# Splitting seven of the fourteen block products of a fused attention and MLP kernel a second time

## The chip, the cores and the metric

The kernel runs on one core of a Trainium2 chip. The core has five engines that run side by side and wait for each other through semaphores: TensorE (PE, matmuls, with its weight loads shown as PEld), VectorE (DVE), ScalarE (ACT), GpSimd (POOL) and SyncE (SP). Each takes its instructions strictly in the order of its own queue, so an instruction that waits holds up all that stand behind it. In this kernel POOL and SP mostly issue transfers. The metric is the device time of one execution in microseconds. Before the change it is 744.53 us, the median of three runs (744.47 to 747.11).

## The reference

The input x has 2048 rows of 1024 numbers in bf16. The output mixes an attention branch and an MLP branch row by row:

```
g = sigmoid((x * gate_w).sum(-1))                  # one number per row
a = attention(x @ wqkv) @ wo                       # 32 heads of 32; each row looks at 8 rows, 2 apart
b = (gelu(x @ w_gate) * (x @ w_up)) @ w_down       # 3584 hidden columns
out = g * a + (1 - g) * b
```

Both branches end in a product with a weight matrix. The kernel joins the two: it stacks the 3584 hidden columns, scaled by 1-g, on the 1024 attention columns, scaled by g, and w_down on wo. So the last stage is one product of 2048 x 4608 by 4608 x 1024.

## The kernel before

**Products by seven.** All large products use the scheme of Strassen in Winograd's form: a product of matrices cut 2 x 2 needs seven block products instead of eight, with sums and differences of blocks formed beforehand and of results afterwards. The last stage cuts each half of the rows (`down(0)` and `down(1)`, 1024 rows each) into left blocks A11, A12, A21, A22 of 512 rows by 2304 columns, and the weights into R11, R12, R21, R22 of 2304 by 512. A block lies in SBUF as 18 rows of 128 x 512. The formed right blocks are T1 = R12-R11, T2 = R22-T1, T3 = R22-R12 and T4 = R21-T2. On the left, S = A21+A22, then S-A11 (called S2 in the change), then A12-S2; A11 becomes A11-A21. One `down` multiplies, in this order: A11 R11, A12 R21, S T1, S2 T2, (A12-S2) R22, (A11-A21) T3, A22 T4. Each is 4 groups (`j`) of 18 matmuls of 128 x 128 by 128 x 512, one group per PSUM bank; `XT` and `VT` name the two sets of four banks.

**The stages in front.** A *unit* is one such product by seven in the earlier stages, of 28 matmuls, and ends on DVE with an addition (L399). Units 0 and 1 are of the MLP, units 2 (`Q0`) to 17 make queries and keys, the next eight the values, the rest gate and up projections. The attention runs on DVE beside the units: products of queries and keys (`qk_mult`, L593), a sum on PE (`reduce_mm`), the softmax, and the weighting of the values (`pv_all`, "PV"), with products (L732) and folds (L739). Query and key pieces at the edge of a half are kept in memory and done later (`spill`). The R combinations T1 to T4 are made in `t_forms` (L835), 36 additions of 1024 elements, and stored to `t_d`.

**Order of the work.** The order on each queue is fixed when the program is built. For each unit, `run_bg` hands out DVE work from background tasks: each step yields its cost, a unit grants about 4.8 us, the task with the smallest priority number goes first, and a task that yields `None` sleeps for one unit. `at` and `at_end` tie calls to a unit; `due` forces a task's end. The hook at `TFE` finishes `t_forms` and calls `load_v`, the load of the value weights for `sums_v` (L542). When `pv_all` is done, it calls `pre_down_2`, which loads A12 and R21. At the start of the last stage `pre_down_3` loads rows 12 and 13 of A11 and A12, the last hidden columns to be made, and `loads` the later blocks as their buffers (`plan`, ten buffers) come free. All these loads are issued by SP.

**DVE in the last stage.** `scale_task` (L867) scales the 12 hidden rows that aren't scaled yet, three instructions of 2048 elements; `comb_task` (L874) forms a combination of blocks, four of 2048 and one of 1024. S-A11 is formed per `j` (L970). Results go through `u2` and `qs`, sums held in SBUF in f32, and out with `add_out` (L937).

Of the kernel before, what the change touches and what calls it, by code (L numbers as in the profile page):

```python
# [67 lines left out]
def kernel(  # L68
# [64 lines left out]
    with tc.manual_schedule(engines={mybir.EngineType.PE, mybir.EngineType.DVE, mybir.EngineType.Activation,  # L133
# [500 lines left out]
        def spill(s):  # L634
            accs, ps = [], []
            temps = [prod_tile() for _ in range(2)]

            def mult(t, dst):
                qk_mult(dst, qb[s][:, t, :], kb[s][:, t, HALO:HALO + AC])

            def add(g, t):
                TT(out=accs[g], in0=accs[g], in1=temps[t % 2], op=ALU.add)  # L642

            for g in range(NT // QG):
                accs.append(prod_tile())
                mult(QG * g, accs[g])
                yield 1.14
                for t in range(1, QG):
                    mult(QG * g + t, temps[t % 2])
                    yield 1.14  # L650
                    if t > 1:
                        add(g, t - 1)
                        yield 1.14
                add(g, QG - 1)
                yield 1.2
            slotq.append(lambda: spill_reduce(s, accs))
# [11 lines left out]
        def softmax(a, cnt, b0, e):  # L668
# [14 lines left out]
            yield 0.55 * cnt + 0.05  # L683
            front.add(a)
            bg(softmax_back(a, cnt, ee, e4, sw, m, bc), 3, now[0] + 1)

        def softmax_back(a, cnt, ee, e4, sw, m, bc):
            nc.scalar.activation(out=ee, in_=ee, func=ACT.Exp, scale=scale)  # L688
            yield None
            while a // BPS not in gated:  # L690
# [25 lines left out]
        def pv_all():  # L716
# [5 lines left out]
            for i, a in enumerate(PVO):  # L722
                if i + 1 < NBLK:
                    while PVO[i + 1] not in ready:
                        yield None
                    pv_load(PVO[i + 1], i + 1)
                if i == 0:
                    yield None
                v, ab, o_ = vb[i % 2], ab_[i % 2], ob_[i % 2]
# [50 lines left out]
        due(Q0 + NT + 1, bg(late_form3(), 1, Q0 + 8))  # L780
        TFE = Q0 + 14
        due(Q0 + 2 * NT, bg(sums_v(), 2, TFE + 1))
        for s in range(2):
# [3 lines left out]
        QE = Q0 + 2 * NT  # L787
        at_end(QE + 1, lambda: (spill_load(0), spill_load(1)))
        bg(spill(0), 4, QE + 3)
        bg(spill(1), 4, QE + 3)  # L790
        bg(pv_all(), 5, QE + 3)

# [38 lines left out]
        def t_forms():  # L831
            for q in range(NQ):
                r11, r12, r21, r22 = tf[q % 3]
                for o_, a, b_ in ((r11, r12, r11), (r12, r22, r12), (r22, r22, r11), (r21, r21, r22)):
                    TT(out=flat(o_), in0=flat(a), in1=flat(b_), op=ALU.subtract)  # L835
                    yield 0.64
                for k, t in enumerate((r11, r22, r12, r21)):
                    nc.gpsimd.dma_start(out=t_d[k][:, NP * q:NP * q + NP, :], in_=t)
                if q + 3 < NQ:
                    tf_load(q + 3)  # L840

        at(Q0 + 1, lambda: [tf_load(q) for q in range(3)])
        tft = bg(t_forms(), 6, Q0 + 2)
        at(TFE, lambda: (tft.finish(), load_v()))

        plan = [dict(A11=4, R11=5, A12=2, R21=3, A21=6, A22=0, S=8, T1=1, T2=9, R22=7, T3=5, T4=3),
                dict(A11=6, R11=1, A12=8, R21=9, A21=2, A22=4, S=0, T1=7, T2=5, R22=3, T3=1, T4=9)]
        u2 = regf(R_U2, 4 * SC).rearrange("p (j n) -> p j n", j=4)
# [60 lines left out]
        def loads(s, *names):  # L909
            B = Bs(s)  # L910
            for k in names:
# [4 lines left out]
                else:  # L916
                    load_T(B[k], int(k[1]))

        def down(s):
            B = Bs(s)  # L920
            last = s == 1
            eng = nc.sync if last else nc.gpsimd
            base = s * SUP
            XT, VT = (6, 7, 0, 1), (5, 2, 3, 4)

# [5 lines left out]
            def emit(ot, c, nh, j):  # L931
                r0 = base + c * SC + j * P
                eng.dma_start(out=o2[r0:r0 + P, nh * SC:(nh + 1) * SC], in_=ot)

# [7 lines left out]
            VP = [bank(VT[j]) for j in range(4)]  # L942
            rest = pieces(scale_task(A21, s, 1, 0, NE_), scale_task(A22, s, 1, 0, NE_), comb_task(S, A21, A22, ALU.add))
            for j in range(4):
                if j > 1 or last:
                    mm(XP[j], A11, B["R11"], j, True)
                else:
                    mm(XP[j], A11, B["R11"], j, True, 0, NK - 2)
                    yield
                    if j == 1:  # L950
                        for jj in range(2):
                            mm(XP[jj], A11, B["R11"], jj, True, NK - 2, NK)
                            nc.scalar.copy(out=u2[:, jj, :], in_=XP[jj])
                if j > 1 or last:
                    nc.scalar.copy(out=u2[:, j, :], in_=XP[j])  # L955
                take(rest, 3)
            run(rest)
            loads(s, "T3")
            for j in range(4):
# [3 lines left out]
                emit(ot, 0, 0, j)  # L963
            loads(s, "T4")
            for j in range(4):
                mm(VP[j], S, B["T1"], j, True)
                nc.scalar.copy(out=qs[:, j, :], in_=VP[j])
            for j in range(4):
                js = slice(j * P, (j + 1) * P)
                TT(out=S[:, :, js], in0=S[:, :, js], in1=A11[:, :, js], op=ALU.subtract)  # L970
            run(comb_task(A12, A12, S, ALU.subtract), comb_task(A11, A11, A21, ALU.subtract))
            if not last:
                loads(1, "A11", "R11")
            for j in range(4):
                mm(XP[j], S, B["T2"], j, True)
                TT(out=u2[:, j, :], in0=XP[j], in1=u2[:, j, :], op=ALU.add)
                TT(out=qs[:, j, :], in0=qs[:, j, :], in1=u2[:, j, :], op=ALU.add)
            if not last:
                loads(1, "A12", "R21")
            for j in range(4):  # L980
                mm(VP[j], A12, B["R22"], j, False)
                add_out(VP[j], u2[:, j, :], 0, 1, j)
            rest = pieces()
            if not last:
                loads(1, "A21", "T1")
                rest = pieces(scale_task(Bs(1)["A11"], 1, 0, 0, NE_), scale_task(Bs(1)["A12"], 1, 0, 0, NE_))
            for j in range(4):
                mm(XP[j], A11, B["T3"], j, True)
                add_out(XP[j], qs[:, j, :], 1, 1, j)
                take(rest, 1)  # L990
            if not last:
                loads(1, "A22", "T2")
            for j in range(4):
                mm(XP[j], A22, B["T4"], j, False)
                add_out(XP[j], u2[:, j, :], 1, 0, j)
                take(rest, 1)
            if not last:
                loads(1, "R22")
            run(rest)
# [4 lines left out]
        def run_last(b):  # L1004
# [9 lines left out]
            prv.p4()  # L1014
            loads(0, "A22", "T1", "T2", "R22")
            for t_ in list(tasks):
# [59 lines left out]
```

## Time and profile before

| | |
|---|---|
| profiled execution | 744.29 us, span 742.5 us |
| TensorE busy | 724.4 us (98%) |
| VectorE busy | 571.5 us (77%) |
| ScalarE busy | 290.9 us (39%) |
| last stage's matmuls (L928) | 1008 issued, 988 recorded, 216.8 us busy |
| last stage, first matmul | 520.40 us |
| data moved | 140.72 MB, 190 GB/s over the span |

The page shares out the busy time of each engine. Its slices cut the span in 40 equal parts with the busy share in tenths. The chain that ended last is followed back from the last instruction, at each step to what released it, so it names the bound. Matmuls are pipelined: a mean of 379 ns for one is the time from its start to its end, and the spacing of a run of them is shorter. Lines of the timeline give start, duration in us, engine, line, operation, output<-input, and how many; a bracket gives the idle time before and what ended it. A line of a table of stretches gives, after the stretch, its length, and the busy time and number of instructions of PE, PEld, DVE, ACT and POOL, then the granted clock, the share of the transfer engines, and GB/s.

### The profile page before, as it was taken

To read this page: it belongs to the slowest core of one execution; us is meant where nothing else is said; L and a number is where in the kernel's file an instruction comes from. 1 tells how busy PE (TensorE), PEld (TensorE's weight loads), DVE (VectorE), ACT (ScalarE), POOL (GpSimd) and SP (SyncE) were. 2 spreads that over 40 slices of the span, in tenths; PEclk is the share of its full clock that TensorE was granted. 3 is DMA by queue.
4 is the path that set the end of the run, shared out by engine and by line. 5 is a ranking of instruction groups with operands and counts; after the bars stand their busy time and mean duration, and the time that the engine had idled before them with its cause. 6 is when DMAs were issued, how large, how long until landed. Compare 5 with 4: busy or idle time off the path is not lost.

```text
span 742.5 us, 9336 instructions
## 1 busy us (share of the span) xinstructions
PE 724.4 (98%) x3498; PEld 356.1 (48%) x3567; DVE 571.5 (77%) x622; ACT 290.9 (39%) x500; POOL 110.8 (15%) x196
## 2 busy tenths in 40 slices
PE   8999999889999999999999999999999999999998
PEld 4466566545544444444444444444444444444443
DVE  3699999898999899999999999995555533606411
ACT  4554445335457655555555555555111000110000
POOL 1234456222211010101010000100010011000000
PEclk9999999999999999999999999999999999999999
DMA  9977784853225526534444743548898799750011
GB/s 280 269 192 248 259 289 143 290 172 115 99 94 145 176 68 197 172 107 152 141 142 152 232 144 114 169 139 273 280 400 325 253 359 396 276 201 30 15 36 36
DMA packets 117486, 140.72 MB, mean 190 GB/s; under 512 B 18704, under 2 KB 101296, under 8 KB 116416
## 3 DMA queue, kind: packets, MB, share of 16 engines
q1 hardware_dynamic: 104128, 101.00, 42.1%
q0 software_dynamic: 13024, 38.59, 15.5%
q8 instruction: 28, 0.46, 0.3%
q10 hardware_dynamic: 288, 0.52, 0.2%
q14 instruction: 18, 0.15, 0.1%
HBM read 98.01 MB, written 39.99 MB: 186 GB/s over the span
## 4 chain that ended last, share of the span: by engine, by line
PE 87%; DVE 5%; issue 1%; ACT 0%; DMA 0%; POOL 0%; another core or an unknown queue 0%; DVEq 0%
PE banks L362 56%; PE banks L928 29%; DVE arena L593 3%; PE banks L598 1%; DVE arena L399 1%; DVE arena L459 1%; DMA gblk<-g_d 0%; DVE arena L642 0%; DVE arena L835 0%; ACT L688 0%; DVE arena L542 0%; PE banks L278 0%; DVE arena L937 0%; ACT arena L688 0%
## 5 line engine op out<-in xcount | busy, mean ns | idle before, releaser
L362 PE MATMUL banks<-arena 128*128 128x512 bf16 x2137 | 472.5, 379 | 11.4 <-DVE arena L399 7.8
L362 PEld LDWEIGHTS <-arena 128*128 128x128 bf16 x2184 | 240.4, 111 | 242.9 <-issue 14.8
L928 PE MATMUL banks<-arena 128*128 128x512 bf16 x988 | 216.8, 379 | 1.1
L928 PEld LDWEIGHTS <-arena 128*128 128x128 bf16 x1008 | 98.6, 98 | 118.9
L399 DVE TENSOR_TENSOR arena<-banks,arena 128x1024 bf16<-128x1024 f32 x78 | 95.2, 1220 | 21.9 <-PE banks L362 17.0
L385 ACT COPY arena<-banks 128x512 f32<-128x512 f32 x78 | 45.8, 587 | 130.8 <-PE banks L362 130.8
L370 ACT CAST arena<-banks 128x512 bf16<-128x512 f32 x102 | 59.8, 586 | 45.1 <-PE banks L362 42.8
L732 DVE TENSOR_TENSOR arena<-arena 128x2048 bf16<-128x2048 bf16 x64 | 76.9, 1219 | 0.4
L593 DVE TENSOR_TENSOR arena<-arena 128x2048 bf16<-128x2048 bf16 x64 | 74.7, 1217 | 0.1
L739 DVE TENSOR_TENSOR arena<-arena 128x2048 bf16<-128x2048 bf16 (+2 forms) x96 | 73.9, 775 | 1.1
L937 DVE TENSOR_TENSOR arena<-banks,arena 128x512 bf16<-128x512 f32 x24 | 16.6, 692 | 67.6 <-PE banks L928 67.6
L256 POOL DMA_DIRECT2D h_d<-arena x28 | 20.1, 718 | 253.5 <-DVE arena L252 209.0
L392 ACT COPY banks<-banks 128x512 f32<-128x512 f32 x78 | 44.5, 571 | 26.6 <-PE banks L362 18.4
L380 ACT COPY banks<-banks 128x512 f32<-128x512 f32 x78 | 45.0, 577 | 13.8 <-PE banks L362 12.4
L970 DVE TENSOR_TENSOR arena<-arena 128x2304 bf16<-128x2304 bf16 x8 | 10.9, 1359 | 42.4 <-PE banks L928 39.9
L319 DVE TENSOR_TENSOR arena<-arena 128x1024 bf16<-128x1024 bf16 x60 | 38.6, 685 | 0.5
L368 ACT ACTIVATE arena<-banks 128x512 bf16<-128x512 f32 x54 | 32.2, 597 | 15.2 <-PE banks L362 14.3
L867 DVE TENSOR_TENSOR arena<-arena,omgrep 128x2048 bf16<-128x2048 bf16 x24 | 28.1, 1217 | 11.3 <-DMA arena<-h_d 11.3
L252 DVE TENSOR_TENSOR arena<-arena 128x2048 bf16<-128x2048 bf16 x28 | 34.0, 1216 | 3.3 <-ACT arena L370 1.9
L955 ACT COPY arena<-banks 128x512 f32<-128x512 f32 x6 | 3.5, 587 | 81.8 <-PE banks L928 81.8
L874 DVE TENSOR_TENSOR arena<-arena 128x2048 bf16<-128x2048 bf16 (+1 forms) x30 | 31.2, 1111 | 0.1
L407 ACT ACTIVATE arena<-arena 128x1024 bf16<-128x1024 bf16 x27 | 28.3, 1049 | 0.0
(76 smaller groups left out, 301.0 us busy)
## 6 DMA issues: line engine op xcount, KB each, us to landing
arena<-t_d SPq DMA_DIRECT2D x8, 2304.0 KB, 13.7
h_d<-arena POOLq DMA_DIRECT2D x28, 512.0 KB, 4.0
arena<-in_B_w_down_dram SPq DMA_DIRECT2D x6, 1792.0 KB, 14.0
arena<-h_d SPq DMA_DIRECT2D x6, 1792.0 KB, 13.5
t_d<-arena POOLq DMA_DIRECT2D x36, 256.0 KB, 4.5
arena<-in_B_w_gate_dram SPq DMA_DIRECT2D x15, 512.0 KB, 5.2
arena<-in_B_w_up_dram SPq DMA_DIRECT2D x15, 512.0 KB, 4.4
arena<-in_B_w_down_dram SPq DMA_DIRECT2D x28, 256.0 KB, 5.8
```

Of the source, the lines that this page charges most:

```text
L252: TT(out=flat(G), in0=flat(G), in1=flat(U), op=ALU.mult)
L319: TT(out=o_, in0=a, in1=b_, op=op)
L362: self.pe = nc.tensor.matmul(ps, lhsT=self.L[form](kt), rhs=rhs[:, kt, :], start=(start and kt == 0), stop=(kt == HK - 1), skip_group_chec ...
L370: nc.scalar.copy(out=o_, in_=i_)
L380: nc.scalar.copy(out=self.Y, in_=self.X)
L385: nc.scalar.copy(out=self.p5s, in_=self.V)
L392: nc.scalar.copy(out=self.Z, in_=self.Y)
L399: TT(out=self.T[:, :, c2s], in0=pair, in1=self.p5s.rearrange("p (o n) -> p o n", o=1).to_broadcast([P, 2, SC]), op=ALU.add)
L593: TT(out=dst, in0=q.rearrange("p (o s) -> p o s", o=1).to_broadcast([P, NWIN, AC]), in1=_win_ap(k, [[-DIL, NWIN], [1, AC]]), op=ALU.mult)
L732: TT(out=prod2[(t // 2) % 2][:, t % 2], in0=ab, in1=_win_ap(v[:, t, HALO:HALO + AC], [[SJ, NJ], [-DIL, NWIN], [1, SJ]]), op=ALU.mult)
L739: TT(out=out_, in0=h(0), in1=h(1), op=ALU.add)
L928: nc.tensor.matmul(ps, lhsT=L[:, i, j * P:(j + 1) * P], rhs=R[:, i, :], start=(start and q == 0), stop=(q == NK - 1), skip_group_check=not ...
```

## The change

Seven of the 14 block products are themselves done by seven: S T1, S2 T2 and A11 T3 in both halves, and A11 R11 in the second. `level2` cuts a left block into quarters of 256 rows by 1152 columns and a right one into 1152 by 256. One product is then 7 x 2 groups of 9 matmuls with 256 columns. `forms_L` and `forms_R` build its eight sums on DVE, four each, in two further buffers (L5 and R5, and so on). The results of the seven add up in place in PSUM: ACT copies quarter results between the halves of banks, one result (`p5d`) goes through SBUF and is added by DVE, and `zero_left` clears the left halves first. S2 is formed as A22-A11 from the already changed A11 and takes A21's buffer; before it was S-A11 in S's own. Before, A22 T4 was added up in the banks that held A11 T3. Now it gets the other banks, VT, and DVE adds A11 T3's banks to `u2` and `u2` to the result. Around it the loads, the buffers, and in the earlier stages the order of the background tasks are arranged anew: `t_forms` stops at unit 14 and goes on after the value units with a priority ahead of PV, `load_v` is called one unit earlier, `spill` waits for the query-key products, the softmax's exponential is a task of its own. The out-stores of the second half go through POOL but for the last block.

```
         def spill(s):
-            accs, ps = [], []
+            while reduced[0] < 2 * NT:
+                yield None
+            accs = []
...
+            bg(softmax_exp(a, cnt, ee, e4, sw, m, bc), 0, now[0] + 1)
...
                 if i == 0:
+                    pv_task[0].prio = 5
+                    tasks.sort(key=lambda t_: t_.prio)
                     yield None
...
-        TFE = Q0 + 14
-        due(Q0 + 2 * NT, bg(sums_v(), 2, TFE + 1))
+        TFE = Q0 + 13
+        due(Q0 + 2 * NT, bg(sums_v(), 2, TFE + 2))
...
-        bg(pv_all(), 5, QE + 3)
+        pv_task = [bg(pv_all(), 4.2, QE + 3)]
...
         def t_forms():
-            for q in range(NQ):
+            q = 0
+            while q < NQ:
+                if now[0] == TFE - 1 and tf_open[0]:
+                    tf_open[0] = False
+                    while now[0] < NQKV + 1:
+                        yield None
+                    for q_ in range(q, min(q + 3, NQ)):
+                        tf_load(q_)
+                    yield None
...
-        at(TFE, lambda: (tft.finish(), load_v()))
...
+        def tf_close():
+            while tf_open[0] and not tft.done:
+                tft.step()
+            tft.prio = 4.5
+            tasks.sort(key=lambda t_: t_.prio)
+            load_v()
+
+        at_end(TFE - 1, tf_close)
...
+        def forms_L(f, b):
+            f = quads(f)
+            q = lambda kh, h: quarter(b, kh, h)
+            for o_, a, b_, op in ((f[:, 0], q(0, 1), q(1, 1), ALU.add), (f[:, 1], f[:, 0], q(0, 0), ALU.subtract),
+                                  (f[:, 2], q(0, 0), q(0, 1), ALU.subtract), (f[:, 3], q(1, 0), f[:, 1], ALU.subtract)):
+                TT(out=o_, in0=a, in1=b_, op=op)
+                yield 1.3
...
+        def level2(bk, L, R, lf, rf):
...
+            cp = lambda d, s_: nc.scalar.copy(out=d, in_=s_)
+            prod(0, 0, lq(0, 0), rq(0, 0), lambda j: cp(c(1, 1, j), c(0, 0, j)))
+            prod(0, 0, lq(0, 1), rq(1, 0))
+            prod(1, 0, lf[:, 0], rf[:, 0], lambda j: cp(p5d[:, j, :], c(1, 0, j)))
+            prod(1, 1, lf[:, 1], rf[:, 1], lambda j: cp(c(0, 1, j), c(1, 1, j)))
+            prod(1, 1, lf[:, 2], rq(0, 1), lambda j: cp(c(1, 0, j), c(1, 1, j)))
+            prod(0, 1, lf[:, 3], rq(1, 1))
+            for i in (1, 0):
+                TT(out=two_banks(bk, i, 1), in0=two_banks(bk, i, 1), in1=p5d, op=ALU.add)
+            prod(1, 0, lq(1, 1), rf[:, 2])
...
         def down(s):
...
+            if last:
+                run(scale_task(A12, s, 0, 0, NE_))
+                level2(XT, A11, B["R11"], B["L1"], B["R1"])
...
+                loads(s, "T2")
+                run(scale_task(A21, s, 1, 0, NE_))
...
+            run(comb_task(A11, A11, A21, ALU.subtract), scale_task(A22, s, 1, 0, NE_), comb_task(S, A21, A22, ALU.add))
             for j in range(4):
                 mm(XP[j], A12, B["R21"], j, False)
...
+            zero_left(VT)
+            run(woven(forms_L(B["L5"], S), forms_R(B["R5"], B["T1"])))
+            run(comb_task(A21, A22, A11, ALU.subtract))
+            S2 = A21
+            zero_left(XT)
+            level2(VT, S, B["T1"], B["L5"], B["R5"])
             for j in range(4):
-                mm(VP[j], S, B["T1"], j, True)
                 nc.scalar.copy(out=qs[:, j, :], in_=VP[j])
-            for j in range(4):
-                js = slice(j * P, (j + 1) * P)
-                TT(out=S[:, :, js], in0=S[:, :, js], in1=A11[:, :, js], op=ALU.subtract)
-            run(comb_task(A12, A12, S, ALU.subtract), comb_task(A11, A11, A21, ALU.subtract))
+            loads(s, "R22", "T3", "T4")
+            run(woven(forms_L(B["L6"], S2), forms_R(B["R6"], B["T2"])))
+            run(comb_task(A12, A12, S2, ALU.subtract))
+            level2(XT, S2, B["T2"], B["L6"], B["R6"])
...
+            zero_left(XT)
+            rest = woven(forms_L(B["L7"], A11), forms_R(B["R7"], B["T3"]))
             for j in range(4):
                 mm(VP[j], A12, B["R22"], j, False)
+                take(rest, 2)
                 add_out(VP[j], u2[:, j, :], 0, 1, j)
...
+            level2(XT, A11, B["T3"], B["L7"], B["R7"])
+            if not last:
+                loads(1, "A12", "R21", "A21", "T1")
             for j in range(4):
-                mm(XP[j], A11, B["T3"], j, True)
                 add_out(XP[j], qs[:, j, :], 1, 1, j)
+                TT(out=u2[:, j, :], in0=XP[j], in1=u2[:, j, :], op=ALU.add)
...
             for j in range(4):
-                mm(XP[j], A22, B["T4"], j, False)
-                add_out(XP[j], u2[:, j, :], 1, 0, j)
+                mm(VP[j], A22, B["T4"], j, True)
+                take(rest, 2)
+                add_out(VP[j], u2[:, j, :], 1, 0, j)
             if not last:
-                loads(1, "R22")
+                loads(1, "A22")
             run(rest)
```

## The prediction

> **What bounds the kernel now.** I read the page's busy table and slices first, then the chain that ended last, then the groups by shape, then the timeline of the last stage, and last the transfer rates in short stretches.
>
> From the page: busy time per engine, and the 40 slices of TensorE and VectorE.
>
> ```profile
> PE 724.4 (98%) x3498; PEld 356.1 (48%) x3567; DVE 571.5 (77%) x622; ACT 290.9 (39%) x500; POOL 110.8 (15%) x196
> PE   8999999889999999999999999999999999999998
> DVE  3699999898999899999999999995555533606411
> ```
>
> PE is full. DVE is full too until slice 27 and half idle after: the last stage, from 520.4 us on, has PE alone as its bound. The chain that ended last says the same, in order of time (start, us, what):
>
> ```profile
> 525.58 10.74 PE banks L928 x49
> 536.32 0.05 issue
> 536.37 10.74 PE banks L928 x49
> ```
>
> 50 matmuls of 512 columns take 10.79 us, so one takes 0.2158 us. The timeline of PE has the one other width, and the longest wait (in the brackets the idle time before it):
>
> ```profile
> 14.52 2.32 PE L209 MATMUL banks<-ident,arena 128*128 128x128 bf16 x32
> 137.26 4.48 PE L362 MATMUL banks<-arena 128*128 128x512 bf16 x19 [2.66 <-DVE arena L399]
> 154.48 4.48 PE L362 MATMUL banks<-arena 128*128 128x512 bf16 x20 [3.40 <-DVE arena L399]
> ```
>
> The timeline of DVE and SP in the last stage gives the prices of the additions and the times of two loads:
>
> ```profile
> 542.85 3.50 DVE L867 TENSOR_TENSOR arena<-arena,omgrep 128x2048 bf16<-128x2048 bf16 x3 [4.17 <-DMA arena<-h_d]
> 546.26 5.22 DVE L874 TENSOR_TENSOR arena<-arena 128x2048 bf16<-128x2048 bf16 x5
> 556.42 1.36 DVE L970 TENSOR_TENSOR arena<-arena 128x2304 bf16<-128x2304 bf16 x1 [4.94 <-PE banks L928]
> ```
>
> ```profile
> 502.07 0.36 SPq L798 DMA_DIRECT2D arena<-h_d  x1
> 522.83 1.52 SPq L798 DMA_DIRECT2D arena<-h_d  x3
> ```
>
> A scaling of 12 rows costs 3.5 us, a block combination 5.2 us, and one addition of 2304 elements 1.36 us alone. In a row each starts some 0.08 us before the one ahead ends (three of 1.22 us take 3.50), so 1.28.
>
> **The early stages.** The order of DVE's instructions shows nine of the eleven R combinations (L835) of units 14 and 15 gone, with three from ahead of them, to units 32 to 34. Before unit 15's addition (L399, 136.0 us) DVE now has five products and no combination, instead of six and four: 4 us less in front of the addition that PE waits 2.66 us for. `load_v` runs one unit earlier, so the 2.23 us for which the V sums waited on it go, and with them most of the 3.40. PE's waits there were 0.59 + 2.66 + 3.40 = 6.65 us; part of the softmax stands earlier in their place. DVE's rows of these four units sum to 34.4 us before and 28.2 after, against some 27 of PE, which leaves about 3; units 32 to 34 get the 12, of 0.66 us each, and may wait 1. I take **-2.5** (ends -5.5 and 0).
>
> **The late load.** The PV folds end in the order three units later: between the additions that began at 509.43 and 515.49 before, instead of ahead of 497.34. Of them DVE has 1.2 us (the addition) and 2.9 us (four folds) left: 509.43 - 2.5 + 4.1 = 511.0. The load of A12 and R21 is called by the last fold and waits for its store; before, it was issued 4.8 us after the fold (497.25 to 502.07), now at 515.8. What stands behind it on SP's queue are rows 12 and 13 of A11, then A12's, then A21. Windows of 2 us show the 4.46 MB moving from 502 to 518:
>
> ```profile
> 516.00:518.00 2.00, 2.00 (x11) 0.87 (x9) 1.97 (x3) 1.17 (x2) 0.00 (x0) 1.00 0.89 308
> 518.00:520.00 2.00, 2.00 (x11) 0.91 (x10) 2.00 (x2) 1.70 (x3) 0.37 (x1) 1.00 0.03 11
> ```
>
> So they end 16 us after the issue, at 531.8, and A11's rows (0.26 MB at some 300 GB/s) land at 532.7. PE reaches them 36 matmuls (16, 4 of the last unit, 16 more) or 7.8 us after the stage's first: 520.4 - 2.5 + 7.8 = 525.7. PE waits **+7** us, where before it waited for nothing. Ends: 0, if the small load is not queued behind the large one, and 9, at the 268 GB/s of 500 to 510 us. I take the queue: A21 landed at 535.17 and A22, issued 2 us behind it, only 7.68 us later, one after the other.
>
> **The split products, on PE.** One block is 72 matmuls of 512 columns, 72 x 0.2158 = 15.54 us. Split, it is 7 products x 2 x 9 = 126 matmuls of 256 columns, which the trace does not show. Low end: half of 0.2158, 0.108. High end: the line between the 128-column row ((2.32 - 0.244)/31 = 0.067 us, with the row's mean of 244 ns) and 0.2158, which is 0.117. I take 0.109: a weight load has 98 ns in L928's row, below 0.108, and the 128-column pairs show that loads follow each other faster still. 126 x 0.109 = 13.73 us; seven blocks: 7 x (15.54 - 13.73) = **-12.6**.
>
> **The forms, on DVE.** Each split adds eight additions of 2304 elements, 8 x 1.28 = 10.3 us, a pair of bank clears (512 elements each; nearest row L144, 256 in 0.27 us: 1.1 the pair) and two additions on banks (L976's 0.68 us: 1.35). Between the end of A11 R11 and the last quarter product of S2 T2, DVE's queue holds per half, in order: A11-A21 5.2, scale A22 3.5, S 5.2, clear 1.1, forms 10.3, S2 5.2, clear 1.1, additions 1.35, forms 10.3, A12-S2 5.2, first addition 0.7: 49.15 us. A11-A21 overwrites A11, so it can't start before PE has left A11 R11. PE has beside it A12 R21 15.54, S T1 13.73, and S2 T2 without its last quarter product 13.73 - 1.96 = 11.77: 41.04. DVE is 8.1 us longer, and it starts late. In half 1 A21 lands at 532.7 + 0.9 (A12's rows) + 7.7 = 541.3, when PE ends A11 R11 (532.7 + 40 x 0.2158 = 541.3), and its scaling of 3.5 is then still to do. In half 2 the scaling stands behind the second addition of the split A11 R11, which comes 1.8 us before that product's end: 0.7 + 3.5 - 1.8 = 2.4 late. PE so waits 8.1 + 3.5 = 11.6 and 8.1 + 2.4 = 10.5: **+22.1**. By places, with lateness o: o - 1.0 at the first clear of S T1; 5.7 at its last quarter product (32.3 + o against PE's 26.6 + o), because S2 stands before the additions; 3.15 at S2 T2's. Ends: 16 (o zero) and 25 (A22's load of half 2, issued as the block before ends, with 26 us of traffic at 355 GB/s called 15.5 us earlier still ahead of it, may cost up to 2).
>
> **What I cost at nothing.** The copies between quarters on ACT (512 columns 0.58; 256 take less) run while PE does the other half of a product, 9 x 0.109 = 0.98 us. The forms for A11 T3 and the next A11 R11 lie beside blocks of 15.5 us with 10.3 + 2.8 of DVE work. The out-stores of half 2 go to POOL, 5.8 us to landing instead of 1.7: the first output of T4 waits some 2.6 us for its tile, on DVE, with a block of 15.5 us to hide it. T4 in its own banks removes no wait, for PE had none; the last output still goes to SP.
>
> **Sum.** The profiled execution took 744.29 us, 1.8 more than its span and 0.24 under the median. 744.3 - 2.5 + 7 - 12.6 + 22.1 = 758.3; I say **758**.
>
> **The rivals.**
> DVE keeps up. If the waits of the two halves sum to under 8.1 instead of 22.1, the kernel is no slower; with none it is 744.3 - 2.5 + 7 - 12.6 = 736. It would need a form at 0.84 us instead of 1.28 (32 of them in the two chains). Against it: 512, 1024, 2048 and 2304 bf16 elements took 0.42, 0.68, 1.22 and 1.36 us, contiguous or not. Chance 0.07.
> A11's rows are not late: 751. Against it the order in which A21 and A22 landed. 0.14.
> Narrow matmuls at 0.117: +1.0 per block. The four blocks inside the chains hide it in their waits; three don't: 761. 0.12.
> PE slow after long waits. The first six matmuls took 630 ns each, 251 over the usual 379, after an idle start; after the wait of 3.40 us, 20 took 4.48 us, the usual time. Waits of 7 and 5.7 us are longer than any seen. At 1.5 us (6 x 0.251) to 4 us (16 of them before full speed at 7.84 us) for each of the three, most is taken back, since 3.15 or 3.5 us of wait for DVE follow each: +2 at the most, 760. 0.08.
> Of the last case the Trainium skill speaks too, page "TensorE: Matmul & The Clock Gate", section Part 1: after an idle window of about 3.4 us the array's clock is halved until it has been busy for as long again. By that rule, as an estimate, each of the three waits could cost up to 1.7 us, before what is taken back; the trace of before has no wait long enough to agree or not.
>
> **How the numbers follow.** The forecast has 0.59. Slower by over 0.5% (3.7 us, about what a measurement of this kernel can tell from no change) are the forecast and all rivals but the first: 0.88 after 0.05 for smaller ends that add up (late load 0 and o zero: 745). Within: 0.05. Faster: 0.07. The range runs from 747 (751 less 4 of lateness) to 766 (758 with 3 for the narrow matmuls, 2 for the load, 3 for slow starts).
>
> **What would show it.** An idle time of about 7 us before an A11 R11 matmul, released by a load of h; 256-column matmuls at 0.109 us; in each half waits on DVE of 1 to 2.5, 5.7 and 3 us in front of split products, 10 to 12 together; DVE without a gap from A11-A21 to the last addition of S2 T2. I am wrong if these waits are absent, or if DVE idles there.

## The result, and the profile after

The changed kernel takes 754.94 us (median of 4 runs, 754.15 to 756.62). The kernel before took 745.82 us on the same chip (4 runs, 744.47 to 747.2). The ratio is 1.0125, with a 95% interval of 1.0094 to 1.0156: slower by 9 us, where 758 was forecast, 13.7 above the profiled execution of before. The profiled execution after took 755.15 us (span 753.3), 10.9 more than that of before; the sums below go from the one to the other.

The page of the kernel after, busy time and slices:

```profile
PE 722.1 (96%) x3945; PEld 394.5 (52%) x3945; DVE 661.3 (88%) x716; ACT 310.6 (41%) x556; POOL 116.9 (16%) x208
PE   8999999999999999999999999998698999997998
DVE  3699999969998999999999999996399989699953
PEclk9999999999999999999999999999799999998999
```

PE's busy time fell by only 2.3 us, although seven blocks were made cheaper. A slice is 18.8 us. PE has a 6 from 527 us on, an 8 from 565 and a 7 from 678; DVE, half idle there before, is full in most of the last stage. The PEclk row dips beside two of PE's three holes.

The groups of the last stage give the same in sums: one row of before, two of after (behind the busy time and the mean the idle time of the engine in front of them, and what ended it):

```profile
L928 PE MATMUL banks<-arena 128*128 128x512 bf16 x988 | 216.8, 379 | 1.1
L1015 PE MATMUL banks<-arena 128*128 128x512 bf16 x504 | 112.1, 384 | 8.6 <-DMA arena<-h_d 8.6
L990 PE MATMUL banks<-arena 128*128 128x256 bf16 x882 | 101.7, 279 | 11.6 <-DVE banks L1003 9.8
```

So 20 us of waits stand where before there was 1.1 in all: 8.6 for a transfer and 11.6 for DVE. PE's timeline shows where (start, us, what, in brackets the idle time before):

```profile
516.53 3.62 PE L1015 MATMUL banks<-arena 128*128 128x512 bf16 x16
520.85 3.62 PE L1015 MATMUL banks<-arena 128*128 128x512 bf16 x16
533.05 26.36 PE L1015 MATMUL banks<-arena 128*128 128x512 bf16 x112 [8.58 <-DMA arena<-h_d]
559.24 11.95 PE L990 MATMUL banks<-arena 128*128 128x256 bf16 x108
574.36 15.58 PE L990 MATMUL banks<-arena 128*128 128x256 bf16 x126 [3.17 <-DVE banks L1003]
590.85 2.13 PE L990 MATMUL banks<-arena 128*128 128x256 bf16 x18 [0.90 <-DVE banks L1003]
608.35 13.92 PE L990 MATMUL banks<-arena 128*128 128x256 bf16 x126
622.11 15.70 PE L1015 MATMUL banks<-arena 128*128 128x512 bf16 x72
668.87 12.23 PE L990 MATMUL banks<-arena 128*128 128x256 bf16 x108 [1.77 <-DVE banks L979]
686.36 16.05 PE L990 MATMUL banks<-arena 128*128 128x256 bf16 x126 [5.25 <-DVE banks L1003]
702.85 2.12 PE L990 MATMUL banks<-arena 128*128 128x256 bf16 x18 [0.44 <-DVE banks L1003]
```

The stage begins at 516.53 instead of 520.40. The row at 608.35 is a split block that waits for nothing: from its start to the next one's is 13.76 us, 0.1092 for each of its 126 matmuls. The rows at 533.05, 574.36 and 686.36 stand behind the long waits, and each is longer than its count: 112 matmuls of 512 columns should be recorded as 24.35 us (at 0.2158, and 0.17 for the last one's own length) and took 26.36; 126 of 256 columns took 15.58 and 16.05 instead of 13.92. In all three the granted clock is 0.50 for a while (532 to 536, 576 to 578 and 686 to 690 us). The row at 668.87 is 0.28 longer than the one at 559.24, but at a granted clock of 1.00: PE stops once more in it, until 677.00, for the third pair of forms.

DVE's timeline in the first half, and two rows of the second:

```profile
539.05 3.50 DVE L894 TENSOR_TENSOR arena<-arena,omgrep 128x2048 bf16<-128x2048 bf16 x3 [11.48 <-DMA arena<-h_d]
542.46 5.23 DVE L901 TENSOR_TENSOR arena<-arena 128x2048 bf16<-128x2048 bf16 x5
567.39 5.24 DVE L901 TENSOR_TENSOR arena<-arena 128x2048 bf16<-128x2048 bf16 x5
572.74 1.03 DVE L979 MEMSET banks<- 128x512 f32 x2
573.66 1.25 DVE L1003 TENSOR_TENSOR banks<-banks,arena 128x512 f32<-128x512 f32 x2
590.08 1.31 DVE L1003 TENSOR_TENSOR banks<-banks,arena 128x512 f32<-128x512 f32 x2
```

```profile
653.64 5.23 DVE L901 TENSOR_TENSOR arena<-arena 128x2048 bf16<-128x2048 bf16 x5
659.59 3.50 DVE L894 TENSOR_TENSOR arena<-arena,omgrep 128x2048 bf16<-128x2048 bf16 x3 [0.71 <-DMA arena<-h_d]
```

DVE first waits 11.48 us for A21 itself, and from A11-A21 (542.46) on has no gap to 590. The two additions at 573.66, for which PE waits at 574.36, stand behind the 5.24 us that form S2 for the next product; those at 590.08 stand behind as much for A12-S2. In the second half the same work runs from 653.64 to 702.8 (the last row of the chain below), with one wait of 0.71 us, for A22's load. SP's timeline and the chain that ended last say why A21 and A11's rows are late:

```profile
514.04 0.36 SPq L805 DMA_DIRECT2D arena<-h_d  x1
524.00 2.75 SPq L805 DMA_DIRECT2D arena<-h_d  x3
```

```profile
526.08 12.95 DMA arena<-h_d
567.49 5.14 DVE arena L901 x5
585.04 5.14 DVE arena L901 x5
702.18 0.62 DVE banks L1003
```

A12's load went out at 514.04 (502.07 before), the two small ones and A21 at 524.00. The chain runs over A21's transfer (12.95 us) and then along DVE until 590.8: no longer along PE. In the second half it passes A22's transfer (18.81 us from 640.76 on) and again DVE, until 702.8.

From these rows, the 10.9 us:

| | predicted | measured |
|---|---|---|
| start of the last stage | -2.5 | 516.53 - 520.40 = -3.9 |
| wait for A11's rows | +7 | 8.6 |
| seven split blocks | -12.6 | 7 x (13.76 - 15.54) = -12.5 |
| waits for DVE, half 1 | +11.6 | 3.17 + 0.90 = 4.1 |
| waits for DVE, half 2 | +10.5 | 1.77 + 5.25 + 0.44 = 7.5 |
| matmuls that took longer than their count behind waits | in a rival | 2.0 + 1.7 + 0.3 + 2.1 = 6.1 |
| gaps counted from a matmul's full length, 6 x 0.16 | | 1.0 |
| sum | +14.0 | +10.9 |

### The profile page after: what moved, and what is told of

Read it like the earlier page. It is cut to its first block, busy times and chain, and to the rows that moved or that the text cites. A ratio compares the mean times of both kernels' runs of the same rounds, so it can differ in the third digit from the quotient of the medians.

```text
span 753.3 us, 10346 instructions
## 1 busy us (share of the span) xinstructions
PE 722.1 (96%) x3945; PEld 394.5 (52%) x3945; DVE 661.3 (88%) x716; ACT 310.6 (41%) x556; POOL 116.9 (16%) x208
## 4 chain that ended last, share of the span: by engine, by line
PE 58%; DVE 15%; DMA 5%; issue 1%; ACT 1%; SPq 0%; DVEq 0%; ACTq 0%
PE banks L362 44%; PE banks L1015 9%; DVE arena L901 5%; PE banks L990 4%; DMA arena<-h_d 4%; DVE arena L967 3%; DVE arena L959 3%; DVE arena L894 1%; DMA arena<-in_B_w_down_dram 1%; DVE arena L593 1%; DVE arena L399 1%; DVE banks L979 1%; DVE banks L1003 0%; PE banks L598 0%; DVE arena L644 0%
## 5 line engine op out<-in xcount | busy, mean ns | idle before, releaser
L362 PE MATMUL banks<-arena 128*128 128x512 bf16 x2184 | 475.4, 379 | 4.8 <-DVE arena L399 3.0
L362 PEld LDWEIGHTS <-arena 128*128 128x128 bf16 x2184 | 240.5, 111 | 239.1 <-issue 11.0
L1015 PE MATMUL banks<-arena 128*128 128x512 bf16 x504 | 112.1, 384 | 8.6 <-DMA arena<-h_d 8.6
L990 PE MATMUL banks<-arena 128*128 128x256 bf16 x882 | 101.7, 279 | 11.6 <-DVE banks L1003 9.8
L399 DVE TENSOR_TENSOR arena<-banks,arena 128x1024 bf16<-128x1024 f32 x78 | 95.3, 1221 | 18.8 <-PE banks L362 11.7
L990 PEld LDWEIGHTS <-arena 128*128 128x128 bf16 x882 | 88.2, 100 | 25.6 <-issue 12.5
L385 ACT COPY arena<-banks 128x512 f32<-128x512 f32 x78 | 45.8, 587 | 130.8 <-PE banks L362 130.8
L1015 PEld LDWEIGHTS <-arena 128*128 128x128 bf16 x504 | 49.7, 99 | 68.8 <-DMA arena<-h_d 9.1
L995 ACT COPY banks<-banks 128x256 f32<-128x256 f32 x42 | 15.0, 357 | 87.9 <-PE banks L990 87.9
L1020 POOL DMA_DIRECT2D out_dram<-arena x28 | 15.2, 543 | 197.6 <-DVE arena L1024 137.3
L901 DVE TENSOR_TENSOR arena<-arena 128x2048 bf16<-128x2048 bf16 (+1 forms) x40 | 41.9, 1120 | 0.0
## 6 DMA issues: line engine op xcount, KB each, us to landing
arena<-in_B_w_down_dram SPq DMA_DIRECT2D x6, 1792.0 KB, 12.6
```

What stands on the lines that cost most here:

```text
L362: self.pe = nc.tensor.matmul(ps, lhsT=self.L[form](kt), rhs=rhs[:, kt, :], start=(start and kt == 0), stop=(kt == HK - 1), skip_group_chec ...
L385: nc.scalar.copy(out=self.p5s, in_=self.V)
L399: TT(out=self.T[:, :, c2s], in0=pair, in1=self.p5s.rearrange("p (o n) -> p o n", o=1).to_broadcast([P, 2, SC]), op=ALU.add)
L901: TT(out=f(o_), in0=f(a), in1=f(b), op=op)
L990: nc.tensor.matmul(c(i, h, j), lhsT=l[:, kt, j * P:(j + 1) * P], rhs=r[:, kt, :], start=False, stop=(kt == KH - 1), skip_group_check=True)
L1015: nc.tensor.matmul(ps, lhsT=L[:, i, j * P:(j + 1) * P], rhs=R[:, i, :], start=(start and q == 0), stop=(q == NK - 1), skip_group_check=not ...
```

## Experiments

Two parts of the change can be had alone: the edits of the early stages, which bring the late load, and the splits in the last stage. Each ratio is to the kernel before, measured beside the run: a median of 745.17 us for the first four runs and 744.23 for the others.

### The early stages alone

The kernel before with the edits of `spill`, `pv_all`, `t_forms`, `TFE` and the wakes, and an unsplit last stage.

```
-            for q in range(NQ):
+            q = 0
+            while q < NQ:
+                if now[0] == TFE - 1 and tf_open[0]:
...
-        bg(pv_all(), 5, QE + 3)
+        pv_task = [bg(pv_all(), 4.2, QE + 3)]
```

> The kernel before with only the edits of the early stages (the background tasks), the last stage unsplit. Theory: the early edits save PE 3.9 us ahead of the last stage (516.53 against 520.40 us for its first matmul) but end PV later, so A11's rows 12 and 13 come 8.6 us late and the matmuls behind that wait run slow for about 2 us more: +6.7 us in all, about 751 us against 744.3, with an idle time of 8 to 9 us in front of the matmuls of A11 R11. The split has no part in it. Rival: the late rows come from the new last stage (its loads), and then this kernel shows no such wait and is about 4 us faster than before, 740.5.

Measured: 751.58 us (6 runs, 751.29 to 754.6), ratio 1.0082 (1.0055 to 1.011). PE's timeline:

```profile
516.38 3.62 PE L953 MATMUL banks<-arena 128*128 128x512 bf16 x16
532.71 213.35 PE L953 MATMUL banks<-arena 128*128 128x512 bf16 x976 [8.39 <-DMA arena<-h_d]
```

The stage starts 4.0 us earlier, PE then waits 8.39 for A11's rows, and the 976 matmuls behind take 2.6 more than at 0.2158 each (210.8). -4.0 + 8.4 + 2.6 + 0.2 = +7.2, and the profiled execution took 751.57, 7.3 more than before. The rival, no such wait and 740.5 us, is out. The late load is real, and the edits of the early stages are a loss by themselves: what they win in front is spent waiting for a load that they also delay.

### The splits alone

The changed kernel with the early stages of before.

```
-        TFE = Q0 + 13
+        TFE = Q0 + 14
...
-        pv_task = [bg(pv_all(), 4.2, QE + 3)]
+        bg(pv_all(), 5, QE + 3)
```

> The changed kernel with the early stages of before: only the split of the last stage. Theory: no wait for A11's rows; the seven splits give 12.5 us back; DVE's queue makes PE wait in both halves, at the last quarter product of S T1 and of S2 T2, some 8 to 10 us per half with the slow matmuls behind the waits counted in: 744.3 - 12.5 + 18 = 750, within 748 to 752. Rival 1: the halves' waits were caused by the late A21, and without it the first half waits nothing: about 741. Rival 2: the loss of the changed kernel is all the late load of A11 (8.6 + 2 us): 744.5.

Measured: 753.52 us (6 runs, 749.68 to 755.85), ratio 1.0103 (1.0069 to 1.0137). PE's timeline, two rows of the early stages and two of the last:

```profile
137.04 6.17 PE L362 MATMUL banks<-arena 128*128 128x512 bf16 x20 [2.65 <-DVE arena L399]
154.75 6.17 PE L362 MATMUL banks<-arena 128*128 128x512 bf16 x20 [2.21 <-DVE arena L399]
572.58 18.73 PE L965 MATMUL banks<-arena 128*128 128x256 bf16 x144 [5.25 <-DVE banks L978]
684.12 15.58 PE L965 MATMUL banks<-arena 128*128 128x256 bf16 x126 [5.25 <-DVE banks L978]
```

Without the late load PE waits in each half for DVE: 0.64 + 5.25 in the first, 1.21 + 5.25 + 0.91 in the second, 13.3 in all, and the matmuls behind lose 5.1 (144 took 18.73 instead of 15.9, 126 took 15.58 instead of 13.92, and twice 108 took 0.3 more). That is 18.3 for the two chains, which the theory put at 18 here, more than the 12.5 saved. The stage also began 1.95 us later than in the profile of before, with the same order of work: the first two rows, 20 matmuls each, took 4.48 there. 744.3 + 1.95 - 12.5 + 18.3 + 1.0 (five gaps, and 0.2 at the end) = 753.0, and the profiled execution took 753.08. The median is 1.5 us above the expected 748 to 752, which is about what the late start cost in the profile. Both rivals (741 and 744.5) are out. So the waits for DVE don't come from the late load; DVE's chain is longer than PE's work beside it.

### The bank additions later

The two additions of a split product (L1003) only touch the halves of banks that its last quarter product doesn't write, so they can stand behind it.

```
-            for i in (1, 0):
-                TT(out=two_banks(bk, i, 1), in0=two_banks(bk, i, 1), in1=p5d, op=ALU.add)
             prod(1, 0, lq(1, 1), rf[:, 2])
+            for i in (1, 0):
+                TT(out=two_banks(bk, i, 1), in0=two_banks(bk, i, 1), in1=p5d, op=ALU.add)
```

> The changed kernel with the two additions on banks issued behind the last quarter product instead of ahead of it; nothing else. That product goes to the left half of its bank, the additions to the right halves. Theory: PE's waits at the last quarter product (3.17 and 5.25, 0.90 and 0.44 us) go, and with them the slow matmuls behind the longer two (1.7 and 2.1 us); PE then waits for the clear and the forms of S2 T2 instead, 2 to 3.5 us in the first half and 4 to 6 in the second. Net 5 to 8 us less: 747 to 750. Rival: DVE's queue is the bound as a whole and only moves the wait to another place: 754 to 755.

Measured: 751.23 us (9 runs, 748.67 to 752.34), ratio 1.0067 (1.0048 to 1.0085). PE's timeline:

```profile
558.85 15.88 PE L990 MATMUL banks<-arena 128*128 128x256 bf16 x144
576.64 11.95 PE L990 MATMUL banks<-arena 128*128 128x256 bf16 x108 [1.90 <-ACT banks L995]
649.29 17.39 PE L1015 MATMUL banks<-arena 128*128 128x512 bf16 x72 [2.12 <-ACT arena L1034]
682.69 2.74 PE L990 MATMUL banks<-arena 128*128 128x256 bf16 x18 [2.20 <-DVE banks L979]
```

The waits on L1003 are gone: S T1 runs through, and 18 matmuls of the next product with it (144 in 15.88). Behind it PE waits for ACT's copies out of the banks (1.90), which now wait for the additions. A new wait of 2.12 appears in the second half: A12 R21 adds to the banks of the split A11 R11, and ACT's copy of these to `u2` now waits for the additions. A wait of 2.20 on a clear follows, and behind it the granted clock is 0.50 from 684 to 690 us: 18 matmuls took 2.74 instead of 2.13, and the next 108, after another wait of 1.36, 13.93 instead of 11.95. So 3.7 us of medians are won, less than the 5 to 8 expected, and the rest has moved: what DVE owes by the end of S2 T2 is unchanged. Where the additions stand explains a part of the loss, not all of it.

### Matmuls in the wait

36 matmuls are put into the wait for A11's rows, so that PE isn't idle there.

```
+                            for _ in range(36):
+                                nc.tensor.matmul(bank(1), lhsT=A11[:, 0, 0:P], rhs=B["R11"][:, 0, :], start=True, stop=True)
```

> The changed kernel with 36 more matmuls of 512 columns (7.8 us, results not used) in PE's queue in front of rows 12 and 13 of A11, so that PE works while it would wait 8.6 us for these rows. Theory: the 112 matmuls behind the wait, which took 26.4 us instead of 24.5, run at 0.2158 us each again, because PE was not idle; the time stays within 1.5 us of the changed kernel (755), since DVE's chain starts with A21's landing and PE gets back what it loses by waiting longer at S T1's last quarter product (3.2 us growing to about 5). Rival 1: the slow matmuls lie on the path that ends last: about 753. Rival 2: they are slow for another reason than the idle time (loads that land at 360 GB/s beside them): they stay slow.

Measured: 755.43 us (4 runs, 754.67 to 755.7), ratio 1.0119 (1.009 to 1.0149). PE's timeline:

```profile
523.70 7.93 PE L1047 MATMUL banks<-arena 128*128 128x512 bf16 x36
532.30 24.35 PE L1015 MATMUL banks<-arena 128*128 128x512 bf16 x112 [0.66 <-DMA arena<-h_d]
574.66 15.47 PE L990 MATMUL banks<-arena 128*128 128x256 bf16 x126 [5.25 <-DVE banks L1003]
```

Two stretches of the kernel after, and one of this kernel (behind the stretch and its length: busy time and instructions of PE, PEld, DVE, ACT and POOL, then the granted clock, the share of the transfer engines, GB/s):

```profile
528.00:530.00 2.00, 0.00 (x0) 0.00 (x0) 0.00 (x0) 0.00 (x0) 0.00 (x0) 0.50 1.09 372
534.00:536.00 2.00, 2.00 (x6) 0.64 (x5) 0.00 (x0) 1.17 (x2) 0.00 (x0) 0.50 1.10 349
```

```profile
534.00:536.00 2.00, 2.00 (x11) 0.90 (x10) 0.00 (x0) 0.01 (x1) 0.00 (x0) 1.00 1.10 349
```

With PE kept busy, the granted clock is 1.00 instead of 0.50 from 534 us on, and the 112 matmuls take 24.35 us instead of 26.36. Loads land at 349 GB/s in both stretches, so they are not the reason. The slow matmuls do come from PE's idleness. But the 2.0 us are not won: the wait at S T1's last quarter grows from 3.17 to 5.25 and the time stays. Behind the load, DVE's chain sets the end, and PE's speed does not.

### S T1 whole, with the early stages of before

The 10.3 us of forms for S T1, with its clears and its additions, are taken out of DVE's chain, and its block is done whole. Five products stay split.

```
-            zero_left(VT)
-            run(woven(forms_L(B["L5"], S), forms_R(B["R5"], B["T1"])))
...
-            level2(VT, S, B["T1"], B["L5"], B["R5"])
             for j in range(4):
+                mm(VP[j], S, B["T1"], j, True)
                 nc.scalar.copy(out=qs[:, j, :], in_=VP[j])
```

> The early stages of before, and the split of the last stage without S T1: five products split (S2 T2 and A11 T3 in both halves, A11 R11 in the second). Theory: from A11-A21 to the first addition of S2 T2, DVE has 36.4 us left in a half (49.15 less forms, clear and additions of S T1), PE 15.54 + 15.54 + 11.77 = 42.85 us beside it, so with DVE 2 to 4 us late no wait remains and no matmul runs slow: 744.3 - 5 x 1.79 = 735.3, within 734 to 738 in the median. Rival: DVE's work is a bound in sum, not by its place; then waits of some us remain and it is 740 or more.

Measured: 736.87 us (6 runs, 736.52 to 739.31), ratio 0.9897 (0.9878 to 0.9916). It is faster than both kernels. PE's timeline:

```profile
525.28 43.33 PE L990 MATMUL banks<-arena 128*128 128x512 bf16 x200
580.62 2.12 PE L965 MATMUL banks<-arena 128*128 128x256 bf16 x18 [0.21 <-DVE banks L978]
684.41 2.13 PE L965 MATMUL banks<-arena 128*128 128x256 bf16 x18 [0.21 <-DVE banks L978]
```

Of the waits for DVE 0.42 us are left. Giving up 2 x 1.78 us of PE's gain takes away 18 us of waits and of slow matmuls behind them. The sum: 744.3 - 5 x 1.78 + 0.4 = 735.8, and the stage began 0.6 later in this execution; the profiled one took 736.89.

### S2 T2 whole instead of S T1

The same number of instructions on every engine as in the last run, but the other product is done whole.

```
-            zero_left(XT)
...
-            run(woven(forms_L(B["L6"], S2), forms_R(B["R6"], B["T2"])))
...
-            level2(XT, S2, B["T2"], B["L6"], B["R6"])
+            for j in range(4):
+                mm(XP[j], S2, B["T2"], j, True)
```

> The same with S2 T2 whole and S T1 split: again five products split, with the same number of instructions on every engine in sum. Theory: it is the place that counts. The additions of S T1 stand behind S2 on DVE's queue as before, so PE's wait of 5.25 us ahead of its last quarter product stays in both halves, with 1.7 us of slow matmuls behind it, and only the wait of 0.4 to 0.9 us at S2 T2 goes: 744.3 - 9 + 14 + 2 = 749 to 752. Rival: two splits fewer free DVE by the same amount in both kernels, and this one is at 736 as well.

Measured: 752.78 us (4 runs, 749.29 to 754.92), ratio 1.0098 (1.0067 to 1.013); the profiled execution was the slowest of them, 754.92. PE's timeline:

```profile
573.12 3.41 PE L965 MATMUL banks<-arena 128*128 128x256 bf16 x18 [4.18 <-DVE banks L978]
684.09 4.00 PE L965 MATMUL banks<-arena 128*128 128x256 bf16 x18 [4.18 <-DVE banks L978]
```

The same amount of work for DVE, in another place, takes 15.9 us more by the medians. In the profiled executions it is 18.0: 2.9 of it arose ahead of the last stage (its first matmul began at 523.88 instead of 520.96), and the other 15 are waits for DVE, 10.2 instead of 0.4, and matmuls that took longer behind them. The waits were expected 1 us longer, and the median is 0.8 above the expected 749 to 752; the rival at 736 is out. Behind S, its forms and S2 the additions of S T1 come 4.18 us late in each half, after 0.71 and 1.09 for the clears. With S T1 whole, the forms of S2 T2 have PE's 31.1 us of A12 R21 and S T1 beside them. It is not DVE's sum but what stands ahead of the first delivery that decides.

### S T1 whole, with the early stages of the change

> The changed kernel, its early stages too, with S T1 whole: five products split. Theory: the late load of A11's rows stays (8.6 us and about 2 us of slow matmuls), the early gain of 3.9 us stays, DVE's waits go: 744.3 - 3.9 + 10.6 - 9 = 742, within 740 to 744, 12 to 13 us below the changed kernel and some 6 us above the one with the early stages of before. Rival: the late A21 leaves DVE behind all the same, and waits of over 3 us stay in the first half: 746 or more.

The edit is the one above, made to the changed kernel. Measured: 742.93 us (10 runs, 741.96 to 744.62), ratio 0.9976 (0.9963 to 0.9989). PE's timeline:

```profile
532.80 42.47 PE L1015 MATMUL banks<-arena 128*128 128x512 bf16 x184 [8.88 <-DMA arena<-h_d]
587.29 2.13 PE L990 MATMUL banks<-arena 128*128 128x256 bf16 x18 [0.22 <-DVE banks L1003]
```

The wait for A11's rows stays (8.88, and 2.6 of slow matmuls behind it: 184 take 39.9 at full speed), those for DVE are gone. Leaving S T1 whole in the changed kernel wins 12 us. With this run the parts stand in a square (profiled executions, us):

| early stages | no split | seven split | five, S T1 whole |
|---|---|---|---|
| of before | 744.29 | 753.08 | 736.89 |
| of the change | 751.57 | 755.15 | 743.32 |

The new early stages cost 7.3 with PE as the bound and 6.4 with five splits, but only 2.1 with seven (4.0 without the 1.95 by which the run of the splits alone began its last stage late). There the late load delays PE while DVE is the one that is late anyway, so a part of it is paid only once. One execution of each doesn't fix how large that part is.

### R21's load behind the small ones

R21 is no longer loaded with A12 but after the rows of A11 and A12.

```
-            load_R(B["R21"], 1, 0)
...
-            loads(0, "A21")
+            loads(0, "R21", "A21")
```

> The changed kernel with the load of R21 issued behind those of A11's and A12's rows 12 and 13 instead of ahead of them; A12's stays ahead, A21's behind all. Theory: the small rows wait in line behind R21, so PE's wait of 8.6 us in front of A11's rows falls below 2 us, and R21 is there in time. But A21 lands no earlier (539 us), so DVE's chain starts where it did, and PE waits those us later, at S T1's clear and last quarter product: 754 to 757. Rival 1: the wait for A11's rows is lost time by itself: 745 to 748. Rival 2: the rows are late for another reason than the line behind R21 (their store), and the wait of 8.6 us stays.

Measured: 758.32 us (4 runs, 758.16 to 759.94), ratio 1.0182 (1.0161 to 1.0203). PE's and DVE's timelines:

```profile
526.28 8.81 PE L1014 MATMUL banks<-arena 128*128 128x512 bf16 x40 [2.23 <-DMA arena<-h_d]
536.02 15.70 PE L1014 MATMUL banks<-arena 128*128 128x512 bf16 x72 [0.94 <-DMA arena<-in_B_w_down_dram]
560.48 14.54 PE L989 MATMUL banks<-arena 128*128 128x256 bf16 x108 [8.76 <-DVE banks L978]
```

```profile
542.65 3.50 DVE L894 TENSOR_TENSOR arena<-arena,omgrep 128x2048 bf16<-128x2048 bf16 x3 [15.51 <-DMA arena<-h_d]
```

The wait for A11's rows falls from 8.58 to 2.23, and their load takes 2.8 to 3.2 us from issue to landing instead of 9.0, so most of the wait was the queue behind R21. The rest is the second rival: their load can go out only when their store has landed. That took 3.1 us in the kernel before, but 8.2 in the kernel after and 8.0 here, with A12's load moving beside it; that this is what slows it is likely, but not shown. But A21, now behind R21, lands at 542.65 instead of 539.05, the chain on DVE starts 3.6 later, PE waits 8.76 at its first clear, and the kernel is 3.4 us slower than the change. The time is above the expected 754 to 757, for which A21 was to land no later and R21 was to be there in time; PE waits 0.94 for it. The wait on PE that is taken away comes back, with A21's delay on top.

## Why the prediction was right

It foresaw the sign, the mechanism and the place of every wait but one (at the first clear of S T1 in half 1 there was none); the time is 3 us below the forecast and inside its range. That it is so close is partly luck, since terms that were off by 5.5 and 3.7 us cancel in part. Of its signs, one came out too high: the waits for DVE were to be 10 to 12 us in each half and were 4.1 and 7.5. Step by step:

**Early stages, -2.5.** -3.9, between the ends given. As the stage then waits for a landing at about the forecast time, this size made no difference: 1.4 us earlier at the start are 1.6 more of waiting.

**Late load, +7.** The rows were to land at 532.7; PE went on at 533.05. Here two errors cancel: the load went out at 514.04 instead of 515.8, and R21's last part landed at 532.3, 18.2 us later instead of 16. The run of the early stages alone and the one with R21 moved show the cause that was named, the queue, for 6.4 of the 8.6 us. The slow store of the rows, behind the rest, was not in the forecast. The rival "A11's rows are not late" (751, chance 0.14) is out.

**Splits, -12.6.** 0.1092 us per matmul against 0.109 taken: -12.5. The rival at 0.117 is out.

**Chains on DVE, +22.1.** DVE's length was right: from A11-A21 to the end of the first addition on S2 T2's banks, 49.15 us were predicted; in half 1 it is 542.46 to 590.73, in half 2 653.64 to 702.7, 48.3 and 49.1, the latter with the 0.71 for A22 in it, for which up to 2 had been allowed. By the prediction's own rows the wait at S T1's last quarter product should have been put at 6.0 instead of 5.7, for the three places to add up to 8.1 + o. Half 2 began 2.24 us late (2.4 predicted), and its waits with the longer matmuls behind them and the gaps are 7.5 + 2.4 + 0.5 = 10.4 (10.5 predicted).

The step that was mis-sized is half 1, and in it the lateness o = 3.5. A21 was put at 541.3 and landed at 539.05, so the chain began at 542.46 instead of 544.8. And PE was later itself: it left A11 R11 at 543.7 (559.24 - 15.54) instead of 541.3, because 2.0 us of slow matmuls followed the load, which the sum left out. So o was -1.2, and waits of 4.1 with 1.7 of slow matmuls and 0.3 of gaps stand where 11.6 were forecast. That makes -5.5; the load with its slow matmuls was 3.7 larger than forecast (8.58 + 2.0 + 0.16 against 7), the start 1.4 better: 14.0 - 5.5 + 3.7 - 1.4 = 10.8. The sentence that A11-A21 can't start before PE has left A11 R11 was wrong too: it started 1.2 us before, on rows that PE was done with, for the combination is made in five instructions. At 541.3 it would not have mattered.

The rival "DVE keeps up" needed waits under 8.1 in the two halves, or 736 with none. In the changed kernel they were 11.6, with 4.1 in longer matmuls behind them; a form took 1.27, not 0.84. The 736.9 of the run with S T1 whole is another sum (five splits, the early stages of before), and that the numbers agree is chance.

**Slow matmuls behind waits** were given 0.08 and +2 at the most, as most is taken back. The chance was too low: they came behind all three long waits, 5.8 us in the profile. The price was about right. The 36 added matmuls won back 2.0 us of slow matmuls and gained nothing. For the other two it is argued from the last wait in each half, which should be 3.15 less the slow time, 1.5 and 1.0, and was still shorter, 0.90 and 0.44. The Trainium skill, page "TensorE: Matmul & The Clock Gate", section Part 1, halves the array's clock after an idle window of about 3.4 us until it has been busy for as long. The granted clock of 0.50 from 528 to 536 us agrees with the halving, and the 2.0 and 2.1 us lost after the waits of 8.58 and 5.25 are somewhat over the 1.7 that was estimated from it. The wait of 3.17, with 1.7 us lost behind it, is shorter than that window.

**At no cost:** ACT's copies (357 ns of 256 columns), the forms of A11 T3 and of the next A11 R11 and T4's output were all hidden, as predicted: no wait of PE names them in the kernel after.

## What to carry to other kernels

A second split saves PE 1.78 us per block and puts 10 to 13 us of work on another engine, so it pays only where that engine has the time before its next delivery: with the same instruction counts, five splits took 736.9 us or 752.8 depending on which product was left whole. Price such work between two points of delivery, not over a stage in which the engine is half idle. Shorter stages in front win nothing if the next stage then waits for a load that the same reordering made later, and a delay of one engine can be partly free while another is already late, so parts should be measured alone and together.

## What the runs showed of the hardware that was not expected

**Short waits can be followed by slow matmuls, and not every time.** In the run of the splits alone, 20 matmuls took 6.17 us instead of 4.48 after waits of 2.65 and of 2.21 us; with the additions later, 72 took 17.39 instead of 15.70 after 2.12. But 20 took 4.48 after 2.66 and after 3.40 in the profile of before, and after 2.65 in the run with S2 T2 whole, where 20 took 7.18 after 3.70. With R21 moved, 126 took the usual 13.91 after 2.94. None followed 1.90. The clock can also fall when PE is already working again: in the run of the splits alone PE went on at 154.75, and the granted clock is 0.80 over 154 to 156 us and 0.50 over the next 2. Waits of 2.1 to 2.7 us are shorter than the idle window of some 3.4 us that the Trainium skill gives (same page and section); here the measurement differs. The Trainium skill's remark there that the window runs freely, so that the cost varies between runs, agrees with a wait of 2.65 us that was followed by slow matmuls in one execution and not in another.

**The same early stages take different times.** Four kernels with identical early stages began the last one at 520.40, 522.35, 520.96 and 523.88 us, mostly by the slow matmuls behind two early waits. The runs of before range from 743.2 to 748.1. That this is the same cause is likely by size, but it wasn't shown run by run.

**Narrow matmuls stream as well as wide ones.** 256 columns take 0.1092 us, 0.0013 over half of 0.2158 (0.16 us per block), with weight loads of 98 to 100 ns fully hidden under them.
